# Gated linear attention into a PReLU network: the off-diagonal products moved past one first-layer bank, and four idle products fewer

## The chip, the core and the metric

The kernel runs on one core of one Trainium2 chip. The time is that of the device in microseconds for one execution; several runs of the same kernel give a median and a range. A profile is one execution taken by the hardware profiler: it has the start and length of every instruction on the engines TensorE (PE, with its weight loads as PEld), VectorE (DVE), ScalarE (ACT), GpSimd (POOL) and SyncE (SP), and the transfers.

## What is computed

A linear attention with a forget gate per channel (batch 4, 8 heads, 768 tokens, 48 channels per head), whose output, with the heads side by side, goes into two dense layers with a PReLU between them (384 to 2048 to 384):

```
f = 1 / (1 + exp(-f_logit))
for t in range(S):
    state = f[:, :, t, :, None] * state + k[:, :, t] (outer) v[:, :, t]
    y[:, :, t] = q[:, :, t] @ state
x = y with heads side by side                    # (3072, 384)
h = x @ w_in
g = max(h, 0) + alpha * min(h, 0)
out = g @ w_out
```

## The kernel before

The recurrence is cut into chunks of 128 tokens (C), each of two halves of 64 (CH), each half of two blocks of 32 (DB). One step of the program takes one chunk of two batch entries (U = 2) with all eight heads, 256 tokens in all; six chunks by two pairs of batch entries make 12 steps. Each step has four stages, written as Python generators that stop at each `yield`:

- `prepare` (key P, line 258) loads q, k, f and v through GpSimd's queue and makes the products of forget gates on ScalarE and VectorE. In every step but the first two it ends with 16 small DMAs on SP's queue (line 427) that lay the transposed keys into `ksn`.
- `carry` (key O, line 432) has two parts. Part one makes the *off-diagonal products*: 32 small matmuls into the PSUM tile `off` (line 444), which couple the two 32-token blocks of a half, and four ScalarE copies of them into the attention matrix A (line 462). Part two makes the *state products*: 32 small matmuls into `pd` (line 484) from `ksn` and the values `vs`, and VectorE operations that carry the state on (`moved`, lines 494 and 498).
- `attend` (key S) has six parts: for each of the two batch entries the products `raw` (line 520) and `qu` (line 535) with VectorE's masked copies out of them (lines 526 and 541); two rounds of ScalarE copies into A (line 563); the output products `py` (line 574), which read A and `vs`; and the copies to y and the DMAs that turn it into `xT`.
- `network` (key n) is the dense part. Its first eight parts are one *first-layer bank* each: six large matmuls into a PSUM bank `ph` (line 618), `neg` on ScalarE (line 623) and `gate` on VectorE (line 625); after every fourth bank VectorE makes four sums S (line 702). Five more parts make the second layer as seven products `pa` to `pe` of eight matmuls each (line 657), with ScalarE's `Csum` (line 668) reading `pa`; one of these tiles is also called `pd`, and in this text pd means the state products. The first step has a plain second layer instead (line 638).

Each of these float32 matmuls is two weight loads and two products in the trace, so a bank is 12 products there, and off or pd is 64. PSUM is split into two large tiles that off, pd, raw, qu and py take in turn, and four banks that the network takes in turn.

The order of the work on TensorE, VectorE and ScalarE is written out by hand: the program goes through a string of keys and runs each named stage up to its next `yield`. The strings `FIRST` serve the first four steps, while weights are loaded; `USUAL` (line 37) serves each later step. In it, S and O belong to step m, n to the network of step m-1, and Q to the preparation of step m+1, and a number repeats a key:

```
USUAL = "S n2 S n O n O n Q n3 Q n Q S3 n Q S n Q n Q n"
```

Each engine runs its instructions in this order, waiting on semaphores where data comes from another engine or a DMA. Eight steps (the fifth to the twelfth) use USUAL with all its keys. `IDLE` (line 27) is the number of small matmuls on constant data with which TensorE begins (line 736); nothing reads their result.

Of the kernel before, what the change touches and what calls it, by code (L numbers as in the profile page):

```python
# [23 lines left out]
NC2 = C // CH  # L24
NB = DB // 4
WP = 768
IDLE = 56
RAWS, LEADS = 5, 4
UP = 2.0 ** 16

# [3 lines left out]
        "n S P n2 S W n W n O Q n3 O S Q n S Q n Q S2 Q n3",  # L34
        "S n3 P S Q S n O n O n4 Q S Q S Q n S Q n Q n2",
)
USUAL = "S n2 S n O n O n Q n3 Q n Q S3 n Q S n Q n Q n"

def flat(first, usual, steps=12):
    out = []  # L40
    left = {}
    for n in range(steps + 1):
        for key in (first[n] if n < len(first) else usual).split():
            for _ in range(int(key[1:] or 1)):
                k = key[0]
                if k in "awbvW":
                    out.append((k,))
                else:
                    m = n - 1 if k == "n" else n + 1 if k == "Q" else n
                    k = "P" if k == "Q" else k  # L50
                    if 0 <= m < steps:
                        out.append((k, m))
    return out

ORDER = flat(FIRST, USUAL)


@with_exitstack
def kernel(
# [674 lines left out]
    with tc.manual_schedule(engines={mybir.EngineType.PE, mybir.EngineType.DVE, mybir.EngineType.Activation}):  # L734
        for _ in range(IDLE):
            nc.tensor.matmul(idle[0:32, 0:8], lhsT=ones[:, 0:32], rhs=ones[:, 0:8], start=True, stop=True)
# [62 lines left out]
```

## Time and profile before

| what | value |
|---|---|
| time, median of 3 runs | 618.38 us (618.32 to 619.0) |
| span of the profiled execution, first to last instruction | 616.6 us |
| around the span, against the median | 1.8 us |
| mean granted TensorE clock | 0.997 of full speed |
| TensorE products, busy | 587.9 us, 95% of the span |
| VectorE / ScalarE / GpSimd, busy | 80% / 40% / 10% |
| off, one product (line 444) | x768, 199 ns |
| pd, one product (line 484) | x768, 213 ns |
| first-layer banks, one product (line 618) | x1152, 383 ns |

The profile lists no total time of its own execution beside the span; the table sets the span against the median of the timed runs. A line of the timeline has the start in us, the length of the group, engine, line, operation, output and inputs, the tile of the array, shapes, and the number of instructions; in brackets at its end stands idle time just before it and what ended it. Products overlap, so lengths in a group don't add up; the distance from start to start does. The lines of the waits have the engine and line that waited, for what, the sum in us, how often, and the longest.

### The profile page before, as it was taken

Reading aid. Unit: us, or ns where it says so; the run is one execution under the profiler, and the core shown is the slowest. Engines: PE = TensorE matmul, PEld = TensorE weight load, DVE = VectorE, ACT = ScalarE, POOL = GpSimd, SP = SyncE. Lnnn points to the kernel's source line nnn. Section 1 sums busy time; section 2 is a strip of 40 time slices with the busy share of each in tenths; the row PEclk is TensorE's granted clock in tenths of the full one; section 3 lists DMA queues with packets and bytes.
Section 4 is the critical chain, followed back from the end, with each engine's and each line's share of the span. In section 5 each row is a group of like instructions: output and inputs, shape, how many; then the busy total and the mean of one; then the engine's idle time right before and its main releaser. Section 6 shows DMA issues by size and latency. Waiting matters only on the chain.

```text
span 616.6 us, 19078 instructions
## 1 busy us (share of the span) xinstructions
PE 587.9 (95%) x8220; PEld 525.1 (85%) x8220; DVE 496.0 (80%) x997; ACT 245.7 (40%) x466; POOL 62.8 (10%) x117
## 2 busy tenths in 40 slices
PE   3568999999999999999999999999999999999997
PEld 3457867898899899899889899899889889889997
DVE  7599898899898798798798798798898889762251
ACT  5687852441641361262261261352352343223110
POOL 9120010001010011001001001001001000000000
PEclk9998999999999999999999999999999999999999
DMA  9965532014414214214313313413413301201000
GB/s 302 368 236 180 161 86 54 35 37 120 89 31 75 70 39 105 67 35 98 78 34 93 83 35 90 86 35 87 89 35 86 89 2 27 55 1 27 27 1 26
DMA packets 68116, 50.43 MB, mean 82 GB/s; under 512 B 47168, under 2 KB 60608, under 8 KB 68032
## 3 DMA queue, kind: packets, MB, share of 16 engines
q1 hardware_dynamic: 56656, 25.01, 15.6%
q0 software_dynamic: 6864, 22.35, 13.0%
q10 hardware_dynamic: 4512, 1.85, 1.7%
q8 instruction: 65, 1.06, 0.7%
q14 instruction: 19, 0.16, 0.1%
HBM read 36.21 MB, written 4.72 MB: 66 GB/s over the span
## 4 chain that ended last, share of the span: by engine, by line
PE 67%; DVE 19%; ACT 9%; issue 4%; DMA 1%; ACTq 0%; SPq 0%; DVEq 0%
PE ph L618 27%; PE pc L657 9%; PE pa L657 6%; PE pd L657 5%; PE pe L657 4%; PE po L638 3%; PE raw L520 3%; DVE gate L625 3%; PE qu L535 3%; ACT A L563 3%; DVE S L702 3%; DVE qd L287 3%; PE py L574 3%; ACT us L314 2%; PE pb L657 2%
## 5 line engine op out<-in xcount | busy, mean ns | idle before, releaser
L618 PE MATMUL ph<-xT,w_in_sb 128*128 128x256 f32 x1152 | 261.2, 383 | 0.7 <-DVE Csum L661 0.7
L618 PEld LDWEIGHTS ph<-xT,w_in_sb 128*128 128x128 f32 x1152 | 215.9, 190 | 33.2 <-issue 2.4
L623 ACT ACTIVATE neg<-ph 128x512 f32<-128x512 f32 x96 | 57.2, 596 | 198.2 <-PE ph L618 157.1
L625 DVE SCALAR_TENSOR_TENSOR gate<-neg,om,ph 128x256 f32<-128x256 f32 x192 | 82.3, 477 | 52.3 <-ACT neg L623 52.1
L657 PE MATMUL pc<-t,S 128*128 128x192 f32 x352 | 61.7, 329 | 0.0
L657 PE MATMUL pa<-w_out_sb,gate 128*128 128x192 f32 x352 | 61.3, 327 | 0.1
L657 PEld LDWEIGHTS pa<-w_out_sb,gate 128*128 128x128 f32 x352 | 57.9, 190 | 1.0 <-DVE gate L625 0.4
L657 PEld LDWEIGHTS pc<-t,S 128*128 128x128 f32 x352 | 57.3, 190 | 0.6
L526 DVE COPY_PREDICATED ad<-mraw,raw 128x256 f32<-128x256 int32 (+1 forms) x96 | 42.4, 441 | 10.7 <-PE raw L520 8.2
L541 DVE COPY_PREDICATED ad<-mquad,qu 128x224 f32<-128x224 int32 (+6 forms) x140 | 42.0, 300 | 6.2
L419 ACT COPY A<-q 48x512 f32<-48x512 f32 x44 | 27.2, 617 | 36.4 <-DVE q L368 35.9
L563 ACT COPY A<-ad 32x256 f32<-32x256 f32 x96 | 38.5, 401 | 1.4
L330 DVE TENSOR_TENSOR us<-us,fs 128x768 f32<-128x768 f32 (+5 forms) x60 | 36.7, 612 | 0.0
L678 ACT ACTIVATE o<-pa 128x192 f32<-128x192 f32 x11 | 3.6, 330 | 75.2 <-PE pa L657 65.4
L661 DVE SCALAR_TENSOR_TENSOR Csum<-pc,Csum 128x192 f32<-128x192 f32 x22 | 7.8, 356 | 29.8 <-PE pc L657 29.6
L574 PEld LDWEIGHTS py<-A,vs 128*64 128x64 f32 x768 | 25.7, 145 | 6.1 <-issue 2.8
L702 DVE TENSOR_TENSOR S<-gate 128x512 f32<-128x512 f32 x44 | 30.3, 688 | 0.8
L574 PE MATMUL py<-A,vs 128*64 128x64 f32 x768 | 28.7, 232 | 1.9 <-ACT vs L500 0.9
L657 PE MATMUL pd<-w_out_sb,S 128*128 128x192 f32 x176 | 30.4, 326 | 0.0
L657 PE MATMUL pb<-t,gate 128*128 128x192 f32 x176 | 30.4, 326 | 0.0
L657 PE MATMUL pe<-w_out_sb,S 128*128 128x192 f32 x176 | 30.4, 326 | 0.0
L520 PEld LDWEIGHTS raw<-qd,k 48*32 48x32 f32 x1536 | 18.5, 109 | 13.5 <-issue 11.1
(101 smaller groups left out, 744.3 us busy)
## 6 DMA issues: line engine op xcount, KB each, us to landing
w_out_raw<-in_w_out SPq DMA_DIRECT2D x8, 767.8 KB, 5.3
w_in_raw<-in_w_in SPq DMA_DIRECT2D x8, 767.2 KB, 12.1
q<-in_qT POOLq DMA_DIRECT2D x11, 512.0 KB, 4.2
f<-in_fT POOLq DMA_DIRECT2D x11, 512.0 KB, 4.5
k<-in_kT POOLq DMA_DIRECT2D x11, 512.0 KB, 4.8
out<-o SPq DMA_DIRECT2D x24, 192.0 KB, 3.0
vs<-in_v POOLq DMA_DIRECT2D x22, 192.0 KB, 4.8
ksn<-kt SPq DMA_DIRECT2D x80, 32.0 KB, 2.0
```

Source lines behind the costliest of these rows:

```text
L330: nc.vector.tensor_tensor(us[:, :, UO[m]:UO[m] + 4 * n].rearrange("p g (i r) -> p g i r", r=4), us[:, :, skip:skip + 4 * n].rearrange("p g ...
L419: nc.scalar.copy(A[halves(cc)[1], :, par * HP:(par + 1) * HP, CH * cc:CH * (cc + 1)], q3[rows(par)].rearrange("p (u h c) s t -> p u h c (s ...
L520: nc.tensor.matmul(raw[DB * j:DB * (j + 1), par, hp * C:hp * C + QW], lhsT=k[r_, g * DB:(g + 1) * DB], rhs=qd[r_, g], start=True, stop=True)
L526: nc.vector.copy_predicated(adu[:, :, :, d:4], mraw[:, d, :, d:4].bitcast(I32).unsqueeze(1).broadcast_to((128, H, NB, n)), rv[:, :, QO[d]: ...
L541: nc.vector.copy_predicated(ad[:, u, :, :, 4 * m:DB], mquad[:, lo:lo + n].bitcast(I32).unsqueeze(1).unsqueeze(1).broadcast_to((128, 2, HP, ...
L563: nc.scalar.copy(A[s_, u, :, s_], ad[s_, u].rearrange("p r h t -> p (r h) t"))
L574: nc.tensor.matmul(py[64 * par:64 * par + 64, u, o:o + CH], lhsT=vs[bp][:, cc, u, hd * D:hd * D + 64], rhs=A[:, u, par * HP + hp, CH * cc: ...
L618: nc.tensor.matmul(ph[:, j * T:(j + 1) * T], lhsT=w_in_sb[:, kt, m * 128:(m + 1) * 128], rhs=xT[:, kt], start=(kt == 0 and j == 0), stop=( ...
L623: nc.scalar.activation(neg, phv, AF.Relu, scale=-1.0)
L625: nc.vector.scalar_tensor_tensor(gate[:, m % NH, m // NH], neg[:, j], om[:, m:m + 1], phv[:, j], ALU.mult, ALU.add)
L657: nc.tensor.matmul(to[:, 0:DH], lhsT=of(f), rhs=by(f), start=(f == 0 and not more), stop=(f == NH - 1), skip_group_check=True)
L702: nc.vector.tensor_tensor(to, x_, y_, op)
```

## The change

In a usual step the first part of `carry` (off and its copies into A) moves behind the fourth first-layer bank, so that it stands directly ahead of the second part (pd). `IDLE` goes from 56 to 52. Nothing else is changed.

```diff
-IDLE = 56
+IDLE = 52
...
-USUAL = "S n2 S n O n O n Q n3 Q n Q S3 n Q S n Q n Q n"
+USUAL = "S n2 S n2 O2 n Q n3 Q n Q S3 n Q S n Q n Q n"
```

## The prediction

> **What bounds the kernel now.** I read the page first (its busy shares and its chain of work), then the TensorE timeline of single steps, then the waits of the usual steps alone, and last the chain inside one step.
>
> ```profile
> PE 587.9 (95%) x8220; PEld 525.1 (85%) x8220; DVE 496.0 (80%) x997; ACT 245.7 (40%) x466; POOL 62.8 (10%) x117
> PE 67%; DVE 19%; ACT 9%; issue 4%; DMA 1%; ACTq 0%; SPq 0%; DVEq 0%
> q8 instruction: 65, 1.06, 0.7%
> ```
>
> TensorE is busy 95% of the span and two thirds of the chain is its own work. The eight usual steps begin at about 196, 243.5, 290.9, 338.3, 385.6, 432.9, 480.3 and 527.8 us: seven periods of 47.4 us. One of them on TensorE:
>
> ```profile
> 292.00 5.45 PE L618 MATMUL ph<-xT,w_in_sb 128*128 128x256 f32 x24
> 297.38 0.92 PE L520 MATMUL raw<-qd,k 48*32 48x80 f32 x64
> ...
> 299.16 2.86 PE L618 MATMUL ph<-xT,w_in_sb 128*128 128x256 f32 x12
> 301.95 0.76 PE L444 MATMUL off<-q,kh 48*32 48x32 f32 x64
> 302.64 2.86 PE L618 MATMUL ph<-xT,w_in_sb 128*128 128x256 f32 x12
> 305.42 0.94 PE L484 MATMUL pd<-vs,ksn 64*48 64x48 f32 x64
> 306.29 10.63 PE L618 MATMUL ph<-xT,w_in_sb 128*128 128x256 f32 x48
> ...
> 322.05 1.27 PE L574 MATMUL py<-A,vs 128*64 128x64 f32 x36
> 323.47 1.03 PE L574 MATMUL py<-A,vs 128*64 128x64 f32 x28 [0.16 <-ACT A L563]
> 324.44 2.87 PE L657 MATMUL pc<-t,S 128*128 128x192 f32 x16
> ```
>
> Each group follows the one before it; the only hole is in py, whose second half waits for ScalarE's copies into A. The waits of 196 to 575 us on TensorE's weight loads say the same:
>
> ```profile
> PEld off L444 <- issue: 2.7, 8, 0.3
> PEld pd L484 <- issue: 2.7, 8, 0.3
> PEld py L574 <- ACT A L563: 1.6, 6, 0.3
> ```
>
> Off and pd each cost a hole of 0.3 us at the weight loads, once per step; py waits for A in most steps. The chain inside the step shows what makes A late:
>
> ```profile
> 302.02 0.69 PE off L444 x50
> 302.71 0.83 PE ph L618 x3
> ...
> 305.58 0.60 ACT neg L623
> 306.19 0.03 issue
> 306.21 0.88 DVE gate L625 x2
> ...
> 313.41 0.86 DVE qd L287
> ...
> 317.98 2.09 ACT us L314 x4
> ...
> 323.47 1.03 PE py L574 x28
> ```
>
> So a second, nearly as long line runs from the bank between off and pd (its neg at 305.58) over VectorE and ScalarE to py. Both lines move with the change.
>
> **The change, part by part, in the step above.**
>
> *Order.* Now: bank, off, bank, pd, banks. Then: bank, bank, off, pd, banks. In both programs the same instructions with the same waits stand on every engine; on TensorE off moves past one bank, on ScalarE its four copies (L462, 1.27 us) past one neg. Nothing moves on VectorE, POOL or SP, and no DMA is issued elsewhere.
>
> *What goes: one switch between large and small products.* A bank with a small group after it lasts 2.79 us (299.16 to 301.95). Two banks in a row last 5.38 (292.00 to 297.38). Two separate ones are 5.58: 0.20 saved. Off's end towards a bank also goes: its last product starts 0.57 after its first, the next bank 0.69 after it, so 0.12.
>
> *What comes: pd's waits, uncovered.* Pd reads ksn, which sixteen DMAs write, so its first four products (of 32) carry waits on many DMA queues; an instruction holds one, and the rest are nine wait instructions of their own on TensorE's sequencer. The trace has them in this step: 302.672, .783, .889, 303.302, .408, .534, .640, .766 and 305.091. One that finds its semaphore ready is followed by the next 0.106 to 0.126 later. The third lasted 0.34, waiting for VectorE's copies out of qu (L541), which ended at 303.2. Less that wait, nine take about 0.98. Now they run under the bank between off and pd, 2.79 us long, and cost nothing. Afterwards that cover is gone, and only what TensorE holds in its queue can hide them. Behind them stand 28 products of pd and the banks, whose neg and gate ScalarE and VectorE then get later.
>
> How far ahead is the sequencer? In the stream of banks at 262.99 a wait instruction comes up with 33 instructions (loads and products) before it unexecuted. After small products it is hardly ahead: the first wait instruction above stands at 302.672, after off's last product (302.52), though 24 instructions of a bank lie between. Before the first bank of the step from 243.5 the waits come up 0.13 us before the last product of qu, and three of them, 0.32 us, stand before the bank; it starts 0.19 after that product. So the cover left is between 0 and 0.13 us; I take 0.05, by the first of these rows, which is off's own.
>
> [...]
>
> Pd from its fourth product to the next bank takes 0.85: in the step from 338.3 the ninth wait held the fourth until 353.10, and the bank came at 353.95. Now pd takes 0.87 from its first.
>
> *Sum for TensorE per step:* -0.20 - 0.12 + 0.98 + 0.85 - 0.87 - 0.05 = +0.59, say 0.6. In the step above: two banks from 299.16 end at 304.54, off's last product starts at 305.1, the waits end at 306.0, and the next bank begins at 306.9 instead of 306.29.
>
> *What the other line gives back.* The neg after the second bank comes 0.9 earlier, since that bank starts at once. VectorE is then ahead until qd (L287), which waits for ScalarE's f and qd copies, and these stand behind the next bank's neg, 0.6 later. In the step from 243.5: those copies end at 265.23 + 0.6 = 265.83, so qd starts 0.16 earlier than its 265.99. From there TensorE leads: Csum (L668) began at 272.46 with pa's end, 272.21, already past; 0.6 later it starts at pa's end plus 0.08, that is 272.89. So A is 0.4 later while py starts 0.6 later, and py's wait shrinks by 0.2. From py's start to pc's it is now 2.36, 2.33, 2.39, 2.08, 2.33, 2.39, 2.37, 2.22 in the eight steps against 2.08 without a wait, so 0.2 can be had in seven: 1.4. In the eighth (338.3) py has no wait because pd lost 0.28 to its DMA; that wait disappears under the other eight. Off's copies into A, behind one more neg, end 15 us before py reads them: nothing.
>
> *Four idle products.* They end at 8.2 us; off of the first step waits for VectorE until 17.6. Ending 0.4 earlier is hidden by that wait: nothing. If it weren't, it would be at most 0.4. They also shift the program: TensorE's instructions come in 65 blocks of 16 KB, about 256 each, and at 25.3 and 30.3 us the first raw products stop for 1.0 and 2.0 us at such a block. Sixteen instructions fewer move the stop within raw, not out of it: zero, with bounds of -1.0 and +1.0, one such stop lost or won.
>
> *Total:* 8 x 0.6 - 1.4 - 0.3 = +3.1. The profiled span of 616.6 becomes 619.7; the median of 618.38 stands 1.8 above the span, so **621.5 us**.
>
> Bounds of the disputed cost: if nothing hides the nine waits and py gives nothing back, 8 x 0.64 = +5.1. If the cover is 0.13, 8 x 0.52 - 1.7 = +2.4. If the queue's 33 instructions cover 33 x 4.4 ns = 0.15 beyond my 0.05, +1.9. If all are hidden, the sign turns (below).
>
> **Rivals.**
>
> *Faster: the sequencer runs through pd's waits while off streams.* For it: in the stream of banks it is 33 instructions ahead, and off and pd are both short and ready. Against it: the wait instructions come up only after off's last product now. Off's end towards pd would then cost about the 0.12 that it has towards a bank: -0.20 on TensorE, and the line over ScalarE gains up to 0.2 more through py. 8 x 0.2 to 8 x 0.4 is -1.6 to -3.1: 615.3 to 616.8. It decides from the point where less than 0.98 - 0.4 = 0.6 us of the waits is left uncovered, that is, where the sequencer is over 0.4 us ahead at off's end.
>
> [...]
>
> *No change:* waits half covered, or py's line giving back what TensorE loses: 617.2 to 619.6. That the edit moves nothing can be excluded; the order of both programs shows the eight moves.
>
> *Slower by more:* pd waits additionally at the end of an instruction block, since off and pd are now 256 small instructions and nine waits on end, used up in 2.4 us. Raw with qu is as long and loses about 0.1 in some steps (qu 1.16 instead of 1.07 at 298.07). At 0.1 to 0.3 in eight steps: 622.3 to 623.9.
>
> **How the numbers follow.** Forecast (waits uncovered, 620.2 to 622.6): 0.62. Slower by more: 0.08. No change: 0.13. Faster: 0.17. The range of 617.0 to 623.5 leaves out most of the faster case and a little above: under 0.2. A measurement of this kernel tells about 0.2%, 1.2 us, from no change; faster by more than that 0.17, within it 0.13, slower 0.70.
>
> **What would show it.** In a usual step of the changed profile: two banks as one group of 24 lasting 5.38, then off, then pd. Right if pd's first products trickle and pd lasts about 1.6 us from first to next bank, or a hole of 0.3 follows off; if py's wait for A shrinks to under 0.1; if the period is 47.7 to 47.8. Wrong if off to the bank after pd lasts about 1.5 in all: then the sequencer was ahead. A change before 100 us would mean that the instruction blocks count after all.

## The result, and the profile after

| kernel | median of 5 runs | lowest to highest | ratio to before (95% interval) |
|---|---|---|---|
| before | 618.32 us | 616.91 to 619.0 | |
| changed | 623.34 us | 620.48 to 625.14 | 1.0075 (1.0048 to 1.0103) |

The change makes the kernel slower. In two later measurements the changed kernel stood at 1.0067 (1.0052 to 1.0082) and 1.0051 (1.0036 to 1.0067); the forecast of 621.5 is 1.0050 of the time before. The profiled execution of the changed kernel took 623.9 us, its span is 622.1, 5.5 longer than before. (Three single executions far outside all others are left out below: one of after_c at 2083.57 us, the one that its profile shows, one of swap4 at 764.0 and one of the kernel before at 765.34.)

First the page of the changed kernel: busy time by engine, the engines' shares of the chain that ended last, and VectorE's qd group with its idle time and what ended that.

```profile
PE 592.1 (95%) x8212; PEld 529.8 (85%) x8212; DVE 497.1 (80%) x997; ACT 246.6 (40%) x466; POOL 63.0 (10%) x117
...
PE 88%; DVE 6%; ACT 3%; issue 2%; DMA 1%; ACTq 0%; DVEq 0%
...
L287 DVE TENSOR_TENSOR qd<-qd,f 128x768 f32<-128x768 f32 (+2 forms) x36 | 27.2, 756 | 6.0 <-ACT qd L282 6.0
```

TensorE's share of the chain was 67% and VectorE's 19%; now they are 88% and 6%. TensorE alone leads the steps. The qd products wait for ScalarE, in all 6.0 us.

Now the same step as before, on TensorE's timeline of the changed kernel:

```profile
302.43 5.45 PE L618 MATMUL ph<-xT,w_in_sb 128*128 128x256 f32 x24
307.81 0.76 PE L444 MATMUL off<-q,kh 48*32 48x32 f32 x64
308.67 1.58 PE L484 MATMUL pd<-vs,ksn 64*48 64x48 f32 x64
310.18 10.63 PE L618 MATMUL ph<-xT,w_in_sb 128*128 128x256 f32 x48
...
325.94 2.16 PE L574 MATMUL py<-A,vs 128*64 128x64 f32 x64
328.03 2.87 PE L657 MATMUL pc<-t,S 128*128 128x192 f32 x16
```

Subtract the starts. The two banks together take 5.38 (302.43 to 307.81), off 0.86 to pd's start, pd 1.51 to the next bank: 7.75. Before, the same stretch had bank to off 2.79, off 0.69, bank to pd 2.78 and pd 0.87, together 7.13. So 0.62 was lost here. Py is now one group of 64 without a hole and reaches pc after 2.09, where it took 2.39.

The waits on the weight loads from 196 to 580 us show where the hole of pd went:

```profile
PEld off L444 <- issue: 2.7, 8, 0.3
PEld pd L484 <- PE off L444: 0.9, 5, 0.2
PEld pd L484 <- issue: 0.2, 1, 0.2
```

Of pd's eight holes for "issue" (2.7 us before) one of 0.2 is left, since a small group stands ahead of it and not a bank. The price of its waits is less a hole than a trickle: in the trace the nine wait instructions stand at 308.346, .457, .562, .688, .794, .920, 309.026, .152 and .257, one every 0.106 to 0.126 us, and the last product of off is at 308.374. In all eight steps each of the nine lasts only 0.05 us, so none of them still waits for a transfer. Pd's first products come one or two at a time between them, and a line of the timeline shows them only as a group that lasts 1.58 instead of 0.94.

Over all usual steps, from py of the fourth step to py of the twelfth, the time was 378.95 and is 381.97: +3.02. The other 2.5 us of the longer span lie before that, where no instruction is moved except by the idle products.

### The profile page after: what moved, and what is told of

It is laid out like the page before. It is cut to its first block, busy times and chain, and to the rows that moved or that the text cites. A ratio compares the mean times of both kernels' runs of the same rounds, so it can differ in the third digit from the quotient of the medians.

```text
span 622.1 us, 19062 instructions
## 1 busy us (share of the span) xinstructions
PE 592.1 (95%) x8212; PEld 529.8 (85%) x8212; DVE 497.1 (80%) x997; ACT 246.6 (40%) x466; POOL 63.0 (10%) x117
## 4 chain that ended last, share of the span: by engine, by line
PE 88%; DVE 6%; ACT 3%; issue 2%; DMA 1%; ACTq 0%; DVEq 0%
PE ph L618 39%; PE pc L657 9%; PE pa L657 8%; PE pd L657 5%; PE pe L657 4%; PE pb L657 4%; PE py L574 4%; PE po L638 3%; PE raw L520 3%; PE qu L535 3%; PE pd L484 3%; PE off L444 1%; PE xt L592 1%; DVE gate L625 1%; DMA f<-in_fT 1%
## 5 line engine op out<-in xcount | busy, mean ns | idle before, releaser
L287 DVE TENSOR_TENSOR qd<-qd,f 128x768 f32<-128x768 f32 (+2 forms) x36 | 27.2, 756 | 6.0 <-ACT qd L282 6.0
L520 PE MATMUL raw<-qd,k 48*32 48x80 f32 x1536 | 24.0, 243 | 7.6 <-issue 4.4
```

The source lines that it names most:

```text
L287: nc.vector.tensor_tensor(qdv[d], qdv[d - 1][:, :, :, 1:5 - d], f[:, :, 1:5 - d].rearrange("p (g i) r -> p g i r", i=NB), ALU.mult)
L520: nc.tensor.matmul(raw[DB * j:DB * (j + 1), par, hp * C:hp * C + QW], lhsT=k[r_, g * DB:(g + 1) * DB], rhs=qd[r_, g], start=True, stop=True)
```

## The experiments

Two theories stood against each other for the 3 us of the usual steps. Mine: pd's nine waits have lost the bank that covered them. The rival: two small groups side by side cost this whatever they wait for, through the change of the array's tile, or because 256 small instructions are used up faster than they are fetched. For the 2.5 us at the beginning the question was whether the idle products do it. Some kernels were run twice, so that they could be compared on one chip as well.

### The two parts alone

`order_only` and its repeat `order_b` are the changed kernel with the old number of idle products; `idle_only` is the kernel before with the new one.

```diff
 order_only, order_b (against the changed kernel)
-IDLE = 52
+IDLE = 56
 idle_only (against the kernel before)
-IDLE = 56
+IDLE = 52
```

> The new order with 56 idle products as before. Theory (pd's nine wait instructions lose their cover): in each of the eight usual steps off to the bank after pd takes 2.37 us as in the changed kernel (0.86 + 1.51), the period is 47.65 to 47.75, and the kernel is 3 us slower than before, 0.4 to 0.5%. Rival (the four idle products are what costs): no slower than before, and the whole difference is in the run with 52 idle products.

> The old order with 52 idle products. Theory: the same as before within 0.2%; the 2.5 us by which the changed kernel's profile was already late before its fourth step come from where the half-clock stretch of TensorE fell in that execution, and will be seen in some executions of either kernel. Rival (the shorter start moves instruction blocks or the clock): 1.5 to 2.5 us slower than before, 0.25 to 0.4%.

> New order, 56 idle products, again, now on one chip beside the same order with 52. Theory (the four idle products do nothing): 0.4 to 0.65% slower than before and equal to the run with 52 within 0.15%. Rival (with the new order 52 costs more): this one 0.2 to 0.35% faster than the one with 52.

Measured: order_only 1.0053 (1.004 to 1.0066), 621.15 us; order_b 1.0057 (1.0042 to 1.0071), 621.34; idle_only 1.0007 (0.9993 to 1.002), 618.27. The timeline of order_only in this step:

```profile
299.56 5.45 PE L618 MATMUL ph<-xT,w_in_sb 128*128 128x256 f32 x24
304.94 0.76 PE L444 MATMUL off<-q,kh 48*32 48x32 f32 x64
305.77 1.58 PE L484 MATMUL pd<-vs,ksn 64*48 64x48 f32 x64
307.28 1.99 PE L618 MATMUL ph<-xT,w_in_sb 128*128 128x256 f32 x8
```

From start to start 5.38, 0.83 and 1.51: the changed kernel's step but for 0.03. From the last product of qu to the bank after pd it is 7.90 to 8.05 in all eight steps of order_only and of the changed kernel, against 7.31 before (7.60 in the one step whose pd waited for a DMA). The order alone costs the time of the usual steps; the idle products don't.

### The changed kernel again

> The changed kernel once more (new order, 52 idle products), beside a run of the one with the new order and 56 on the same conditions as the other kernels of this set. Theory: its usual steps are those of the new order with 56 idle products, so 2.5 to 3.5 us slower than before (0.4 to 0.55%); what its first runs showed above that came from the start, which differs from execution to execution. Rival: the idle products and the order together cost more than the order alone, 4.5 us or more (0.7%).

> New order, 52 idle products, on the same chip. Theory: equal to the one with 56 within 0.15%. Rival: 0.2 to 0.35% slower than it.

Measured: 1.0067 (1.0052 to 1.0082), 621.52 us, and 1.0051 (1.0036 to 1.0067), 620.91 us. The first alone doesn't decide between theory (at most 0.55%) and rival (0.7%). But side by side on one chip, order_b and after_c are 1.0057 and 1.0051, with intervals that overlap almost wholly. The profile of after_again has the usual steps of the changed kernel (333.88 us from py of step 5 to py of step 12 in both; 331.59 before), but its fourth step's py is at 179.92, as before, and not at 182.41. So +5.5 wasn't what the change costs in every execution.

### The two small groups exchanged: swap

Here both groups still stand side by side behind two banks, with the same instructions and waits, but pd comes first. Its waits then come up under the bank, and off, which needs one wait, follows it. Both kernels have 56 idle products; the edit is shown against the kernel before.

```diff
-USUAL = "S n2 S n O n O n Q n3 Q n Q S3 n Q S n Q n Q n"
+USUAL = "S n2 S n2 O2 n Q n3 Q n Q S3 n Q S n Q n Q n"
...
+        def state():
+            pd = pair(f"pd_{i}")
...
+            return pd
+
         off = pair(f"off_{i}")
+        if c >= 2:
+            pd = state()
...
         yield
-        pd = pair(f"pd_{i}")
...
+        if c < 2:
+            pd = state()
```

> 56 idle products, the new order, but in the usual steps the state products stand ahead of off instead of behind it: bank, bank, pd, off. Off and pd are still 256 small instructions on end with two tile modes side by side; only the nine waits now stand behind a bank's 24 instructions. Theory: the waits are covered, off and pd together cost about 0.2 us less per step than before, and py's wait shrinks: 1.6 to 3.1 us faster than before, 0.25 to 0.5%. Rival (two small groups side by side cost by themselves, by the instruction blocks or by the change of tile): as slow as the changed order, 2 to 3 us slower than before.

> State products ahead of off, 56 idle products, on the same chip. Theory: 0.3 to 0.5% faster than before, equal to the run with 52 within 0.15%. Rival: 0.2 to 0.35% faster than the one with 52, as the first two runs had it.

Measured: 0.9957 (0.9944 to 0.9971), 615.3 us, and 0.9953 (0.994 to 0.9966), 614.98 us. It is faster than both kernels, as the theory had it for both runs. Its timeline:

```profile
298.05 5.45 PE L626 MATMUL ph<-xT,w_in_sb 128*128 128x256 f32 x24
303.42 0.94 PE L446 MATMUL pd<-vs,ksn 64*48 64x48 f32 x64
304.29 0.76 PE L461 MATMUL off<-q,kh 48*32 48x32 f32 x64
304.98 1.78 PE L626 MATMUL ph<-xT,w_in_sb 128*128 128x256 f32 x7
...
321.18 2.15 PE L582 MATMUL py<-A,vs 128*64 128x64 f32 x64
323.25 2.87 PE L665 MATMUL pc<-t,S 128*128 128x192 f32 x16
```

5.37, 0.87 and 0.69 make 6.93, which is 0.20 less than before: exactly the switch that is saved. Pd and off have the durations that they had between banks. In the trace all nine waits are past before pd starts at 303.42 (the last six from 302.345 to 303.102, under the bank), and off's own wait stands at 304.036, before pd's last product. The change of tile costs no more here than at a bank: pd's last product, 304.154, is 0.135 ahead of off's first, and in all eight steps of the kernel before it is 0.135 ahead of the bank. Seven of the eight steps are as short; in the eighth step of the program, as in the kernel before, pd waits 0.29 for a transfer (in swap_b three steps lose 0.14 to 0.29 in pd). The rival that two small groups cost the time by themselves falls.

### The waits taken under the bank by an added product: prewait

The order of the changed kernel is kept, off first, but one product of 128x128 weights and 96 columns is added ahead of off. It reads parts of ksn that all sixteen DMAs write, so that the waits become its own. Its result is written to columns that nothing reads.

```diff
         off = pair(f"off_{i}")
+        if c >= 2:
+            x["pd"] = pair(f"pd_{i}")
+            both = x["ksn"][:, 0, 0:128].rearrange("p (r x) -> p r x", r=2)[:, :, 0:D]
+            nc.tensor.matmul(x["pd"][:, 0, 400:496].rearrange("p (r x) -> p r x", r=2), lhsT=ident, rhs=both, start=True, stop=True)
...
-        pd = pair(f"pd_{i}")
+        pd = x["pd"] if c >= 2 else pair(f"pd_{i}")
```

> 56 idle products, the new order with off ahead of pd, and one more product (128x128 with 96 columns, result not read) between the second bank and off, which reads ksn and so takes the waits on its DMAs before off. Theory: the waits run under the bank; the hole between off and pd's fourth product goes, and the added product costs 0.2 to 0.3 us; off to the bank after pd about 1.6 us plus that product; 0 to 2 us faster than before. Rival (side by side costs by itself): 2 to 4 us slower than before.

Measured: 1.0009 (1.0 to 1.0019), 618.91 us; the expected gain didn't come. The timeline of a step in which it works, and below it the added product of a step in which it doesn't:

```profile
299.60 5.45 PE L622 MATMUL ph<-xT,w_in_sb 128*128 128x256 f32 x24
304.88 0.36 PE L440 MATMUL pd<-ksn,ident 128*128 128x96 f32 x2
305.17 0.76 PE L448 MATMUL off<-q,kh 48*32 48x32 f32 x64
305.86 0.94 PE L488 MATMUL pd<-vs,ksn 64*48 64x48 f32 x64
306.72 10.75 PE L622 MATMUL ph<-xT,w_in_sb 128*128 128x256 f32 x48
...
352.80 0.43 PE L440 MATMUL pd<-ksn,ident 128*128 128x96 f32 x2 [0.58 <-DMA ksn<-kt]
```

In the first, off takes 0.69 and pd 0.86 to the next bank: with its waits gone from between them, pd behind off is as short as behind a bank, and the change of tile from off to pd costs nothing more either. The added product costs 0.19 (5.57 from bank to off instead of 5.38), so the step is at 7.31, as before. That holds in four of the eight steps. In three others (7.65, 8.02 and 8.13) the waits come up late, under little cover, or the added product itself waits; in the 352.80 line it waits for a transfer into ksn. The last (7.90) is another matter: its waits are covered, but the bank behind pd starts 0.52 late. The profile puts that down to ScalarE's copies out of off, which in the seven other steps end after the bank has begun; the section on the prediction comes back to it. The mechanism is shown in the four steps; the remedy isn't worth its price, as it asks for all transfers earlier than pd alone does.

### A part of the waits: half

The added product reads only what the first eight DMAs write. Four wait instructions stay with pd, behind off.

```diff
+            nc.tensor.matmul(x["pd"][:, 0, 400:448], lhsT=ident, rhs=x["ksn"][:, 0, 0:D], start=True, stop=True)
```

> New order with off ahead of pd, 56 idle products, and the added product ahead of off now reads only the half of ksn that the first eight DMAs write; five of pd's nine wait instructions go or move ahead of off, four stay behind off. Theory (each uncovered wait instruction costs 0.106 to 0.126 us): from the last qu to the bank after pd 7.5 to 7.7 us per usual step, between the 7.31 of the kernel with all waits taken ahead and the 7.92 of the changed order; 0.5 to 2.5 us slower than before. Rival (any wait between off and pd costs the whole hole, whatever the number): 7.9 to 8.2 and 4 us or more slower.

Measured: 1.0013 (1.0004 to 1.0022), 619.03 us. Its timeline:

```profile
297.91 5.45 PE L621 MATMUL ph<-xT,w_in_sb 128*128 128x256 f32 x24
303.20 0.32 PE L439 MATMUL pd<-ksn,ident 128*128 128x48 f32 x2
303.44 0.76 PE L447 MATMUL off<-q,kh 48*32 48x32 f32 x64
304.13 1.17 PE L487 MATMUL pd<-vs,ksn 64*48 64x48 f32 x64
305.23 10.87 PE L621 MATMUL ph<-xT,w_in_sb 128*128 128x256 f32 x48
```

Off with pd takes 1.79 here (303.44 to 305.23). It took 1.55 in prewait with no wait left behind off, and 2.37 in the changed kernel with nine. So four waits cost 0.24 and nine 0.82: the loss grows with the number of waits left uncovered, while the products of off and pd and their order are the same in all three kernels. The four cost less than 4 x 0.106, so by that price about two of them are hidden; with nine the first one and a half are. From the last qu to the bank seven of the eight steps take 7.50 to 7.66, as expected; in the last, at 8.28, pd stops for 0.54 with no semaphore behind it.

### Fewer idle products with the exchanged order, and the fourth step

`swap52` and `swap52_b` are swap with 52 idle products. `swap4` exchanges the two groups in the fourth step too.

```diff
 swap52, swap52_b (against swap)
-IDLE = 56
+IDLE = 52
 swap4 (against swap)
-        "S n3 P S Q S n O n O n4 Q S Q S Q n S Q n Q n2",
+        "S n3 P S Q S n2 O2 n4 Q S Q S Q n S Q n Q n2",
...
-        if c >= 2:
+        if bp + c >= 2:
...
-        if c < 2:
+        if bp + c < 2:
```

> State products ahead of off, 52 idle products. Theory: as with 56, about 0.4% faster than before. Rival (fewer idle products cost when the order is new): 0.2 to 0.3% less gain.

> State products ahead of off, 52 idle products, on the same chip. Theory: 0.3 to 0.5% faster than before. Rival: 0.05 to 0.2% faster than before, as in its first runs.

> State products ahead of off in the usual steps and in the fourth step too, where off moves next to pd as well; 56 idle products. Theory: 0.2 from the switch and up to 0.4 from py in one more step, so 0.4 to 0.6 us faster than with the usual steps alone, 0.45 to 0.55% faster than before; no more than the measurement can tell. Rival: the fourth step's pd waits for its transfers, and nothing is gained.

Measured: swap4 0.9947 (0.9931 to 0.9963), 615.16 us, which can't be told from swap. Its profile shows the fourth step at 7.11 instead of 7.31 on TensorE, while py still waits 0.29 for A, so little can reach the end.

Swap52 gave 0.999 (0.9976 to 1.0003), 616.87 us, and swap52_b 0.9975 (0.9963 to 0.9987), 615.91 us: in both, less gain than swap, on one chip 0.9975 against 0.9953. That is the rival of these expectations, and theory missed. The profile of swap52 shows one place, in the middle of off in the eighth step:

```profile
351.75 0.66 PE L461 MATMUL off<-q,kh 48*32 48x32 f32 x52
353.09 0.32 PE L461 MATMUL off<-q,kh 48*32 48x32 f32 x12 [0.68 <-issue]
```

Off stops for 0.68 with no semaphore behind it, and goes on with its twelve last products. In swap52_b the stop isn't seen; its eighth step is nearly as long (7.92 against 8.01 us), but there the last transfer into ksn lands at 350.71, after pd's start at 350.28, and pd takes 1.67. What such stops are, the next section says.

## Why the prediction was right, and where it was not

**The uncovered waits: shown.** The sum for TensorE was +0.6 per step; measured, 7.31 became 7.90 to 7.93 (once 8.05, with a gap of 0.26 between two of the waits, whose cause is open). Term by term in the step shown: two banks in a row save 0.20, as in the forecast (5.38 against 5.58); off and pd take 2.37 instead of 1.56, so +0.81, where off's end, the waits and pd's end less the lead made -0.12 + 0.98 + 0.85 - 0.87 - 0.05 = +0.79. The lead of the sequencer at the end of off, the number with the least behind it, was taken as 0.05; the first wait stands at 308.346 and off's last product at 308.374, so it is 0.03. From that product to the next bank it took 1.81, forecast 1.78. And order_only, swap and half set the number of uncovered waits to nine, none and four: the time follows.

The forecast's one wait per instruction is what the traces of before and of the changed kernel show for TensorE's loads and products: none has more than one (365 loads have one). Of the 248 wait instructions 91 have two.

The bound of +1.9 let the 33 instructions, at an estimated 4.4 ns each (off's 0.57 us over its 128 loads and products), hide 0.15 us more per step, which would then have lost 0.45 instead of 0.6. No run shows such a lead behind off; the measurement decides for the smaller one.

**What py gives back: right in kind, 0.2 us more in sum.** From py's start to pc's start the steps now take 2.08 or 2.09, and 2.22 in the last. Before they took 2.08 to 2.39. The sum given back is 1.62, forecast 1.4. In the timeline above py has no hole, and no wait of py for A is left among the waits of 196 to 580 us. VectorE waits for ScalarE's qd copies, as expected:

```profile
316.49 0.96 DVE L287 TENSOR_TENSOR qd<-qd,f 128x768 f32<-128x768 f32 x1 [0.72 <-ACT qd L282]
```

That wait of 0.72 also says how early VectorE is, and that ScalarE's copies hold it here.

**The usual steps: +3.02, forecast +3.1.** From py of step 5 to py of step 12 the changed kernel takes 333.88, or 47.70 per step; forecast were 47.7 to 47.8.

**The rivals.** The faster one needed the sequencer to be 0.4 us ahead at the end of off; it is 0.03 ahead. But what this rival priced exists: where the waits are covered, swap gains 0.20 per step on TensorE and what py's wait gives back, 1.6 and 1.7 over the eight steps; from end to end it is 3.09 us from py of step 4 to py of step 12 (375.86 against 378.95), and its 614.98 to 615.3 us lie at or just below that rival's 615.3 to 616.8. The change of tile between pd and off takes nothing from this gain: the 0.135 us there is what stands ahead of a bank too. That pd waits additionally at instruction blocks is not seen in the changed kernel's usual steps, none of which is above 8.05, but half has such a stop in pd (0.54) and swap52 one in off (0.68).

**The idle products: the step that was wrong.** They were put at zero, with bounds of -1.0 and +1.0, and a change before 100 us was to show that blocks count. There was one, of 2.5 us at py of the fourth step. What the idle products save is hidden as forecast: the first step's off waits 9.96 us for VectorE instead of 9.38. Of the 2.5 us, 0.70 stand at py of the first step, 0.45 of them from longer stops among raw's products (1.10 and 2.29 us against 0.97 and 1.97), and 2.38 at py of the second. The stretch between the two, in the kernel before and, in the second fence, the changed one:

```profile
43.24 2.83 PE L592 MATMUL xt<-y,dense 128*128 128x256 f32 x12 [1.69 <-ACT y L583]
...
51.57 0.69 PE L454 MATMUL off<-us 48*32 48x16 f32 x54 [1.36 <-issue]
52.38 1.97 PE L471 MATMUL pk<-ident,ks 128*128 128x128 f32 x8
```

```profile
43.73 5.46 PE L592 MATMUL xt<-y,dense 128*128 128x256 f32 x12 [1.71 <-ACT y L583]
...
54.35 0.57 PE L454 MATMUL off<-us 48*32 48x16 f32 x46 [0.82 <-issue]
...
60.41 0.32 PE L520 MATMUL raw<-qd,k 48*32 48x80 f32 x2 [1.05 <-issue]
```

The same twelve xt products take 5.46 instead of 2.83, at a median of 634 ns instead of 379. That isn't the idle products' doing: four of the eight profiles with 56 have 4.35 to 4.88 here (order_only 4.88), and the kernel before has its slow stretch a little later, in pk among others (a granted clock of 0.83 from 50 to 60 us, where the changed kernel's is 1.00; the record has 0.50 for 3.41 us from 52.0). Nor is the first stop behind "issue" a loss: it stands in the kernel before as well, and is longer there (1.36 against 0.82). It stood behind 74 of 128 products before and stands behind 82 now: eight products and their eight loads, the sixteen instructions that were taken out. New is the second stop, of 1.05, behind 62 of raw's 64 products. It is seen in three of the five profiles with 52 idle products (1.05, 0.50 and 1.15 us) and, eight products earlier (0.66), in one of the eight with 56.

That these stops belong to the instruction blocks can be counted. Queue q8 of both pages, of the kind "instruction", brings 65 transfers of 16 KB, one for every 256 or so of the 16688 instructions recorded for TensorE before (16672 now). In these two profiles the weight loads have seven of the stops, and each ends 1.29 to 1.49 us after the end of one of those transfers. Numbered along TensorE's recorded stream (loads, products and wait instructions), the 46 places in the thirteen profiles where the weight loads of a running group stand still for over 0.25 us with no semaphore behind it all come 193 or 194 instructions after a multiple of 256. The stops of swap52's off and half's pd are among them, and the late bank of prewait's last step stands at 193 as well. So the places are fixed in the stream, and the edit moves other products onto them; most such places pass without a stop (a profile has 65 blocks), and how long one lasts differs from execution to execution.

In the times the four products don't show as a shift of the median, as idle_only and the pair order_b and after_c say, but as a tail. Of 51 runs with 52 idle products, over all orders, nine lie more than 1.5 us above the median of their kernel in that series (idle_only up to 621.72, swap52 up to 619.78). Of 116 with 56, the kernel before among them, one does. The first measurement of the changed kernel had three of its five runs at 623.3 to 625.1 and two at 620.5 and 620.6, which is what lifted its median by 2 us over the forecast, to 623.34, just inside the range that ends at 623.5. Staying inside it was luck: nothing in the forecast stood for these 2 us, and the later measurements (621.52 and 620.91) are the ones that its sum describes. That the tail goes with the four products is what the counts show. That the moved stops make it is not shown: the one profile of an execution above 623 us has 1.05 us of a new stop, but swap52_b's has 1.15 us at the same place, in a run that is among the fastest of its twelve (615.25). The zero was right for the median run and wrong for the upper end.

**Open.** Why runs with 52 idle products have the tail, and why swap loses 0.2% with them while the other orders lose nothing at the median: from py of step 4 to py of step 12 the profiles of swap and swap_b take 375.86 and 375.70 us, those of swap52 and swap52_b 376.19 and 375.88, so the usual steps hold little of it. And what decides where in an execution the stretch of slow products at 43 to 56 us falls: the record of the granted clock shows it in the kernel before (0.50 from 52.0 to 55.4), but in the changed kernel it has no entry ahead of 49.76, and the slow xt products stand from 43.73.

## What to carry to other kernels

Count the wait instructions that stand ahead of a group of small products, as well as what they wait for: a tensor written by sixteen DMAs needed nine here, and even when everything had landed they cost about 0.11 us each (0.106 to 0.126 from one to the next) unless large products were still running ahead of them: in swap, behind two banks, all nine were past before pd began. Put the group with the many waits directly behind the large products and the group with few waits behind it; of the two orders of the same two groups here, one lost 0.5% and the other gained 0.45% (with 52 idle products 0.1 to 0.25%). When a kernel has stops that are tied to positions in the instruction stream, look at the spread of the runs as well as the median after any edit that shifts the stream.

## What was not expected of the hardware

A change of tile between two groups of small products cost 0.135 us from the last product of the one to the first of the other, no more than from small products to a bank (0.12 behind off, 0.135 behind pd). The 0.20 that is saved per step is thus the price of going from large products to small ones, and the second small group's hole of 0.3 at the weight loads goes with it (pd's in the changed kernel, off's in swap).

Under most banks the crossing from one block of 256 instructions to the next shows no stop: in the profiles of before and of the changed kernel none over 0.25 us stands inside a bank, and the longest in all profiles is 0.45 us, in swap at 307. Among small products, of which 256 instructions took 1.56 us (pd and off in swap) to 2.37 us (off and pd in the changed kernel), stops of up to 2.3 us were seen, nearly all in the first two steps, while the transfers take 0.51 to 1.03 of the DMA engines' time (the changed kernel from 50 to 60 and from 24 to 33 us). Two stand in the usual steps where that share is 0.00 (0.68 in swap52 from 352.4, 0.54 in half from 541.9).
